# Values' products spread over the steps, value matrices loaded at the end of the bias stage, and six row buffers in an attention and two-layer expert kernel

## The chip, the cores and the metric

The kernel runs on one core of a Trainium2 chip. The metric is the device time of one execution in microseconds (us), the median over runs. Five engines work side by side, each through its own list of instructions in order: TensorE (PE, with its weight loads PEld), VectorE (DVE), ScalarE (ACT), GpSimd (POOL) and SyncE (SP). SP here does nothing but issue DMA transfers.

## The reference

Two batches, eight heads, 576 positions, head size 64. The attention scores get an additive bias that a small network computes from the distance of two positions; two layers of a 1152-token feed-forward block follow.

```
scores = scale * np.matmul(q, k.transpose(0, 1, 3, 2))
rel = (pos[:, None] - pos[None, :]).astype(np.float32)
psi_rel = np.log1p(np.abs(rel))
psi_i = np.log1p(np.maximum(pos[:, None].astype(np.float32), 1.0))
x = (psi_rel / psi_i)[..., None]
h = np.maximum(x @ w1 + b1, 0.0)
bias = h @ w2
scores = scores + bias.transpose(2, 0, 1)[None, :, :, :]
attn = np.exp(scores - np.max(scores, axis=-1, keepdims=True))
attn = attn / (np.sum(attn, axis=-1, keepdims=True) + 1e-09)
out = np.matmul(attn, v)
...
h = x @ w_in
g = h * (1.0 / (1.0 + np.exp(-1.702 * h)))
x = g @ w_out
...
h = x @ w_in
P = a[0] + a[1] * h + a[2] * h2 + a[3] * h3
Q = 1.0 + np.abs(b[0]) * np.abs(h) + np.abs(b[1]) * h2
out = (P / (Q + 1e-06)) @ w_out
```

## The kernel before

The order of all work is written out by hand; nothing reorders it. Each engine runs its own instructions in the order in which the code below emits them.

**Bias stage: beats.** The bias is made in 36 rows of 16 query positions (`A.rows`). A row goes through three functions, one beat apart. `bias_hidden` fills four hidden tiles (`room`) on DVE, POOL and ACT. `bias_matmul` multiplies them on PE into a PSUM tile, `wide` or `narrow`. `bias_out` copies the result to a tile `st` in SBUF with ACT (for three rows DVE, L141), mirrors the rest of the row with ACT, DVE or POOL, and SP writes `st` to the DRAM array `bias_all` (L152). `st` has four buffers: a fifth row waits until the write of the row four before it has landed. `beat()` is called from the step loop, with `FIRST[s]` saying how many beats stand ahead of step `s`, so that steps 0 to 9 lie between the beats. Beats also load the bias back for the steps (`bias_load`, tiles `bt`), prepare the first heads' queries and keys (`load_qk`, `q_high`, `k_low` and so on) and load the value matrices of the first three pairs (`load_v`).

**Attention: steps.** There are 40 steps. A step (`hp`, `b`, `qc`) is a pair of heads, a batch and one of five blocks of queries, in the order 4, 0, 1, 2, 3; block 4 has both heads in one tile, so half the matmuls. In step `s` PE does: the tail transposes of step `s - 3` (`tails`, L281 to L292, into a corner of the `wide` tiles that the scores of step `s` then use), the scores (L216), the other transposes of step `s - 3` into two PSUM tiles `pt`, and some parts of the values' products (`values`, L370 and L373). Scores use `wide`, of which there are two; DVE's L236 adds the bias, finds the extreme and frees the tile. ACT takes the exponentials (L240), copies `pt` to SBUF tiles `PT` (`evacuate`), and copies finished products (`xt`) to the input of the feed-forward block (L390); DVE's L395 makes the low part of these.

**Values.** A group is three blocks (4, 0, 1; 320 queries) or two (2, 3; 256 queries) of one pair of heads. When its last block has been evacuated, five parts are put on the list `pv`: parts 0 to 3 are two matmuls each (L370), part 4 is one (L373), after which the product is complete. The piece `pv` of a step takes parts from that list. From step 12 on it stands ahead of the evacuations in a step. Two `PT` tiles alternate, so the evacuations of a group wait for the products of the group two before it.

**Feed-forward.** From step 40 on the same loop lets the first hidden products of the feed-forward block (L485) start; its weights are split into two parts by `conv` pieces (L447 to L474), of which 14 stand in the attention steps listed in `CONVS`. The rest of the program is the feed-forward block (L485, L566, L573).

Of the kernel before, what the change touches and what calls it, by code (L numbers as in the profile page):

```python
# [24 lines left out]

QORDER = (4, 0, 1, 2, 3)
GROUPS = (((0, 256, 0), (512, 64, 256)), ((256, 256, 0),))
RLAG = 0

NFULL = 10  # L30

TLAG = 3
CONVS = (1,3,4,6,7,8,9,11,12,16,17,18,19,21)

FIRST = (19, 19, 21, 26, 30, 30, 39, 39, 39, 41, 41)

# [16 lines left out]
class Attention:  # L53
# [72 lines left out]

    def bias_out(self, r):
        nc = self.nc
        st = self.bp.tile([128, BW], F32, tag="st", name="st", bufs=4)
        c = int(self.rows.index(r) not in GP3)  # L130
        ps, left = self.bps.pop(r), 16 * r + 15
        n = ps.shape[1]

        if r < 18:
            side, other, image = st[:, left:], st[:, 0:left], st[:, 2 * left:left:-1]
        else:
            side, other, image = st[:, 0:n], st[:, n:], st[:, left - 1:left - (S - 16 * r):-1]
        i = self.rows.index(r)
        scale, bias = self.bc[:, C_NI + r:C_NI + r + 1], self.corr[:, c:c + 1]
        if i in (19, 28, 29):  # L140
            nc.vector.tensor_scalar(out=side, in0=ps, scalar1=scale, scalar2=bias, op0=ALU.mult, op1=ALU.add)  # L141
        else:
            nc.scalar.activation(out=side, in_=ps, func=AF.Identity, scale=scale, bias=bias)  # L143
        if i in (2, 3, 4, 7, 10, 13, 15, 18, 19, 21, 23, 24, 31, 32, 35):
            nc.scalar.copy(other, image)
        elif i in (8, 12, 14):
            nc.vector.tensor_copy(other, image)
        else:
            nc.gpsimd.tensor_scalar(out=other, in0=image, scalar1=1.0, scalar2=1.0, op0=ALU.mult, op1=ALU.mult)
# [34 lines left out]
        self.k[pb] = p.tile([128, 2, S], F32R, tag="k", name="k", bufs=bufs)  # L184

    def q_high(self, pb):
        self.nc.gpsimd.tensor_scalar(out=self.q[pb][:, 0, :], in0=self.raw[pb][:, 0:QW], scalar1=1.0, scalar2=1.0,
                                     op0=ALU.mult, op1=ALU.mult)

    def q_low(self, pb, a, b):  # L190
# [2 lines left out]
                                     op=ALU.subtract)  # L193

    def k_high(self, pb):
        self.nc.scalar.activation(out=self.k[pb][:, 0, :], in_=self.raw[pb][:, QW:], func=AF.Copy, scale=-0.125)

    def k_low(self, pb):
        k = self.k[pb]
        self.nc.vector.scalar_tensor_tensor(out=k[:, 1, :], in0=self.raw[pb][:, QW:], scalar=-0.125,  # L200
                                            in1=k[:, 0, :].bitcast(F32), op0=ALU.mult, op1=ALU.subtract)


# [90 lines left out]
    def tails_out(self, s):  # L294
        if not 0 <= s < len(self.steps):
            return
        hp, b, qc = self.steps[s]
        PTt = self.PT[hp, b, int(qc in (2, 3))][1]
        copy = self.nc.scalar.copy if qc in (() if hp else ()) else self.nc.vector.tensor_copy
        if qc < 4:  # L300
            o = 128 * (qc % 2)
            if isinstance(self.tl, list):
                for i in range(2):
                    copy(PTt[:, o + 64 * i:o + 64 * i + 64], self.tl[i])
            else:
                copy(PTt[:, o:o + 128], self.tl)
        else:
            for a in range(2):
                sl = slice(64 * a, 64 * a + 64)
                copy(PTt[sl, 256:320], self.tl[a][0:64, :])  # L310

    def transposes(self, s):
        self.evacuate(0)
        self.evacuate(1)
        if not 0 <= s < len(self.steps):
            return
        nc = self.nc
        hp, b, qc = self.steps[s]
        p = self.P.pop(s)
        off = 128 * (qc % 2) if qc < 4 else 256  # L320
        self.ev = (hp, b, int(qc in (2, 3))), qc, off, [], s < NFULL and qc < 4
        pts = self.ev[3]
        for i in range(2):
            pt = self.pt.tile([128, 512], F32, tag=f"pt{i}", name="pt", bufs=1)
            pts.append(pt[:].rearrange("p (a c q) -> p a c q", a=2, c=4))
        for a in range(2 if qc < 4 else 1):
            for c in range(4):
                x = p[:, a, 128 * c + 64 * a:128 * c + 64 * a + 128]
                if qc == 4:
                    for i in range(2):  # L330
                        sl, o = slice(64 * i, 64 * i + 64), 128 * c + 64 * i
                        nc.tensor.transpose(pts[i][:, a, c, :], p[sl, a, o:o + 128], self.ident[sl, sl], tile_position=(64 * i, 0))
                elif s < NFULL:
                    nc.tensor.transpose(pts[a].rearrange("p a c q -> p (a c q)")[:, 128 * c:128 * c + 128], x, self.ident)  # L334
                else:
                    self.flip([pt[:, a, c, :] for pt in pts], x)


    def evacuate(self, i):
        if self.ev is None:  # L340
# [5 lines left out]
        copy = nc.scalar.copy if i or qc in eva else nc.vector.tensor_copy  # L346
# [7 lines left out]
        if i and qc in (1, 3):  # L354
            self.pv += [(grp, c) for c in range(5)]
        self.ev = None if i else self.ev


    def values(self, grp, c):
# [17 lines left out]
    def values_out(self):  # L377
        nc = self.nc
        if self.xt is None:
            return  # L380
        (hp, b, g), n, xt = self.xt
        self.xt = None
        for q, m, o in GROUPS[g]:
            end = b * S + q + m
            while m:
                ci, i = divmod(end - m, CH)
                w = min(m, CH - i)
                hi, lo = self.x[ci]
                self.xlo.append((lo[:, hp, i:i + w], xt[:, o:o + w], hi[:, hp, i:i + w]))
                nc.scalar.copy(hi[:, hp, i:i + w], xt[:, o:o + w])  # L390
                m, o = m - w, o + w

    def values_lo(self):
# [5 lines left out]
class Moe:  # L399
# [68 lines left out]
    def split(self):  # L468
        if self.ready:
            nc = self.nc  # L470
            w, o, val, j = self.ready
            self.ready = None
            nc.scalar.copy(w[:, 2 * o, :], val)  # L473
# [103 lines left out]
def attention_moe_moe(tc, t):  # L577
# [50 lines left out]
    def beat():  # L628
# [20 lines left out]
            A.k_high(i // 10)  # L649
        if i in (7, 14):  # L650
            A.k_low(i // 10)
        if i in (21, 26, 34):
            A.load_v((21, 26, 34).index(i))
        if i in (14, 16, 18, 22):
            A.load_qk(2, (14, 16, 18, 22).index(i))
        if i == 7:
# [14 lines left out]
    g, nh = {}, 0  # L671
    for s in range(n + TLAG + 2):
        prep = []
        while s <= 10 and beats[0] < FIRST[s]:
            beat()
        if s < n:
# [14 lines left out]
        else:  # L691
            A.values_out()
            A.values_lo()
            A.tails(s - TLAG)
        if s == n:
            A.ps.release()
# [11 lines left out]
        for piece in (('ea','eb','xa','to','qh','ql','kh','xb','su','cv','pv','tr','no','vo','kl','vl') if s < 12 else ('tr','vo','to','pv','qh','ea','ql','kh','eb','xa','xb','su','no','kl','vl','cv')):  # L708
            if piece == 'ea':
                A.evacuate(0)  # L710
            elif piece == 'eb':
                A.evacuate(1)
            elif piece == 'su':
                A.sums(s - 1)
            elif piece == 'to':
# [27 lines left out]
            elif piece == 'tr':  # L743
                A.transposes(s - TLAG)
            elif piece == 'pv':
                for _ in range(5 if s >= n or len(pv) > 5 else 2 if pv and pv[0][1] == 0 else 3):
                    if pv and s >= 10:
                        A.values(*pv.pop(0))
                if s == n + TLAG + 1 and 1:
# [247 lines left out]
```

## Time and profile before

| | before |
|---|---|
| median of 3 runs | 595.82 us (595.65 to 596.84) |
| profiled execution | 597.2 us, span 595.3 us |
| PE busy | 569.3 us (96% of the span) |
| ACT, DVE, POOL busy | 439.9, 422.5, 379.6 us |
| chain that ended last | PE 78%, DVE 7%, ACT 6%, DMA 4%, POOL 3%, issue 2% |

Busy shares are averages over stages with different limits. The bias stage takes the span's first 75 us or so, the attention steps without beats run to about 179 us, and the feed-forward block takes the rest. In the rows further down, the first number of a timeline row is the start in us from the span's start.

### The profile page before, as it was taken

The page shows a single profiled execution, that of the slowest core. Times are in us where ns is not written, and L with a number is a line of the kernel's source. Part 1 is how long each engine was busy: PE and PEld are TensorE (multiplying, and loading weights), DVE is VectorE, ACT ScalarE, POOL GpSimd, SP SyncE. Part 2 cuts the span into 40 slices and gives each one's busy share as a digit, 9 for nine tenths or more (in the row PEclk, how much of TensorE's full clock was granted, in tenths as well). Part 3 has the DMA queues.
Part 4 walks back from the last instruction along what each step waited for, and adds up shares of the span by engine and source line. Part 5 has one row for each costly group of instructions (what it writes and reads, how often), then busy time and mean ns, then how long its engine had stood idle before and what let it go on. Part 6 is the DMA issues. An engine that isn't in the chain of part 4 may idle for free.

```text
span 595.3 us, 10998 instructions
## 1 busy us (share of the span) xinstructions
PE 569.3 (96%) x3815; PEld 480.1 (81%) x3815; DVE 422.5 (71%) x919; ACT 439.9 (74%) x929; POOL 379.6 (64%) x431
## 2 busy tenths in 40 slices
PE   6986999999999999999999999999999999999997
PEld 2233466666666999999999999988898989999995
DVE  7987775688876886565655737678998666657663
ACT  7987777898987675555545536779999887888783
POOL 5957554577755775546554646759888665656563
PEclk9987999999999999999999999999999999999999
DMA  5789760834514564343443414501200100010001
GB/s 170 208 277 283 223 247 2 317 133 143 196 59 142 177 196 150 115 130 123 139 126 122 139 41 138 179 1 35 72 1 1 54 1 2 0 37 19 0 1 53
DMA packets 23911, 66.25 MB, mean 111 GB/s; under 512 B 2480, under 2 KB 3376, under 8 KB 23856
## 3 DMA queue, kind: packets, MB, share of 16 engines
q1 hardware_dynamic: 23712, 65.43, 34.0%
q8 instruction: 30, 0.49, 0.3%
q14 instruction: 25, 0.20, 0.1%
q10 hardware_dynamic: 144, 0.13, 0.1%
HBM read 52.30 MB, written 13.25 MB: 110 GB/s over the span
## 4 chain that ended last, share of the span: by engine, by line
PE 78%; DVE 7%; ACT 6%; DMA 4%; POOL 3%; issue 2%; SPq 0%; ACTq 0%; POOLq 0%; DVEq 0%
PE hps L485 30%; PE acc L566 16%; PE acc L573 15%; PE wide L216 5%; PE xt L370 4%; DVE p L236 3%; PE wide L123 2%; DMA bt<-bias_all 2%; PE pt L334 1%; PE pt L292 1%; PE xt L373 1%; DMA bias_all<-st 1%; PE narrow L123 1%; PE wide L292 1%; ACT st L143 1%
## 5 line engine op out<-in xcount | busy, mean ns | idle before, releaser
L485 PE MATMUL hps<-xhi,w 128*128 128x384 f32 x768 | 150.8, 337 | 0.9 <-DVE part L547 0.9
L485 PEld LDWEIGHTS hps<-xhi,w 128*128 128x128 f32 x768 | 135.6, 188 | 6.7 <-DVE part L547 2.7
L497 POOL TENSOR_TENSOR glo<-sg,ghi 128x384 fp32r<-128x384 f32 x48 | 49.0, 1020 | 72.5 <-PE acc L566 50.0
L474 POOL TENSOR_TENSOR w<-tmp,w 128x512 fp32r<-128x512 f32 x64 | 85.4, 1334 | 10.4 <-ACT w L473 10.0
L252 POOL TENSOR_SCALAR p<-p,mn 128x576 f32<-128x576 f32 x72 | 59.0, 829 | 47.0 <-DVE mn L250 39.6
L485 PE MATMUL hps<-xlo,w 128*128 128x384 f32 x384 | 82.0, 334 | 0.0
L566 PE MATMUL acc<-ghi,w 128*128 128x384 f32 x384 | 78.4, 334 | 0.1
L573 PE MATMUL acc<-w,ghi 128*128 128x512 f32 x288 | 75.8, 393 | 0.0
L485 PEld LDWEIGHTS hps<-xlo,w 128*128 128x128 f32 x384 | 68.0, 188 | 0.0
L566 PEld LDWEIGHTS acc<-ghi,w 128*128 128x128 f32 x384 | 67.6, 188 | 0.4 <-DVE xlo L395 0.4
L504 DVE TENSOR_TENSOR sg<-hps,sg 128x384 f32<-128x384 f32 x48 | 26.7, 557 | 51.9 <-ACT sg L503 51.9
L544 POOL TENSOR_SCALAR ra<-ra,small 128x384 f32<-128x384 f32 x48 | 28.2, 587 | 55.1 <-ACT ra L529 55.0
L240 ACT ACTIVATE p<-p,mn 128x576 f32<-128x576 f32 x72 | 55.7, 779 | 9.7 <-DVE mn L236 9.5
L573 PEld LDWEIGHTS acc<-w,ghi 128*128 128x128 f32 x288 | 53.4, 188 | 8.6
L236 DVE CUSTOM_DVE_ANT_0 p<-wide,bt 128x576 f32<-128x576 f32 x72 | 52.3, 751 | 9.3 <-PE wide L216 6.3
L494 ACT CAST ghi<-sg 128x384 fp32r<-128x384 f32 x48 | 24.7, 514 | 43.3 <-PE acc L566 27.2
L546 POOL TENSOR_TENSOR ra<-ra,part 128x384 f32<-128x384 f32 x48 | 49.9, 1039 | 4.0
L216 PE MATMUL wide<-k,q 64*128 64x288 f32 (+1 forms) x432 | 46.2, 318 | 2.2 <-ACT st L143 1.7
L503 ACT ACTIVATE sg<-hps 128x384 f32<-128x384 f32 x48 | 23.5, 489 | 30.6 <-PE hps L485 30.6
L566 PE MATMUL acc<-glo,w 128*128 128x384 f32 x192 | 45.0, 334 | 0.0
L447 ACT ACTIVATE up<-raw 128x512 int32<-128x512 uint32 x59 | 37.5, 636 | 7.5 <-DVE tmp L463 6.6
L573 PE MATMUL acc<-w,glo 128*128 128x512 f32 x144 | 42.5, 393 | 0.0
(115 smaller groups left out, 1158.3 us busy)
## 6 DMA issues: line engine op xcount, KB each, us to landing
raw<-win SPq DMA_DIRECT2D x32, 512.0 KB, 3.6
raw<-wout SPq DMA_DIRECT2D x32, 512.0 KB, 3.5
bias_all<-st SPq DMA_DIRECT2D x36, 295.5 KB, 3.7
bt<-bias_all SPq DMA_DIRECT2D x16, 576.0 KB, 5.9
qk<-qk SPq DMA_DIRECT2D x7, 608.0 KB, 6.3
v<-v SPq DMA_DIRECT2D x8, 320.0 KB, 5.6
out<-o SPq DMA_DIRECT2D x8, 256.0 KB, 2.2
bt<-bias_all SPq DMA_DIRECT2D x8, 144.0 KB, 3.6
```

What stands on the lines that cost most here:

```text
L216: nc.tensor.matmul(ps[:, half, 0:288], q[p, x, 128 * qc:128 * qc + 128], k[p, y, 288 * half:288 * half + 288], start=(i == 0), stop=(i == ...
L236: nc.vector.tensor_tensor_reduce(out=pv.rearrange("p (x j) -> p x j", x=2), in0=ps[:, :, 0:288], in1=self.bt[qc][:, a, :].rearrange("p (x ...
L240: nc.scalar.activation(out=pv, in_=pv, func=AF.Exp, bias=mn[:, a:a + 1], scale=-1.0, accum_out=mn[:, 2 + 2 * a:3 + 2 * a])
L252: nc.gpsimd.tensor_scalar(out=p[:, a, :], in0=p[:, a, :], scalar1=mn[:, 8 + a:9 + a], scalar2=1.0, op0=ALU.mult, op1=ALU.mult)
L447: nc.scalar.activation(out=self.up[j].bitcast(I32), in_=lo, func=AF.Copy, scale=2.0 ** -29)
L474: nc.gpsimd.tensor_tensor(out=w[:, 2 * o + 1, :], in0=val, in1=w[:, 2 * o, :].bitcast(F32), op=ALU.subtract)
L485: nc.tensor.matmul(ps[:, 0:CH], w[:, wi, 128 * d:128 * d + 128], xx[:, d, :], start=(i == 0 and d == 0), stop=(i == 2 and d == 3))
L497: nc.gpsimd.tensor_tensor(out=glo[:], in0=g, in1=ghi[:].bitcast(F32), op=ALU.subtract)
L544: nc.gpsimd.tensor_scalar(out=t0[0][:], in0=t0[0][:], scalar1=self.pb[:, 1:2], scalar2=1.000001, op0=ALU.mult, op1=ALU.add)
L546: nc.gpsimd.tensor_tensor(out=t0[0][:], in0=t0[0][:], in1=t0[1][:], op=ALU.add)
L566: nc.tensor.matmul(acc[e][:, 0:CH], w[:, wi, 128 * e:128 * e + 128], g[gi][:], start=(first and i == 0), stop=(last and i == 2))
L573: nc.tensor.matmul(acc[e][:], g[gi][:, 128 * e:128 * e + 128], w[:, wi, :], start=(first and i == 0), stop=(last and i == 2))
```

## The change

Four things change, beside a number of switches that are added and left off (`KLE`, `QHE`, `TACT` and so on), and a bookkeeping list in `evacuate` that leaves the order as it was.

```
-        st = self.bp.tile([128, BW], F32, tag="st", name="st", bufs=4)
+        st = self.bp.tile([128, BW], F32, tag="st", name="st", bufs=6)
...
-        if i in (21, 26, 34):
-            A.load_v((21, 26, 34).index(i))
+        if i in (38, 39, 40):
+            A.load_v((38, 39, 40).index(i))
...
-                for _ in range(5 if s >= n or len(pv) > 5 else 2 if pv and pv[0][1] == 0 else 3):
+                for _ in range(5 if s >= n else 3 if len(pv) > 5 else 2):
                     if pv and s >= 10:
                         A.values(*pv.pop(0))
...
-CONVS = (1,3,4,6,7,8,9,11,12,16,17,18,19,21)
+CONVS = (1, 3, 4, 5, 6, 7, 8, 9, 11, 12, 16, 17, 18, 19, 21)
```

Rows for the bias wait on the write of the row six before them, no longer four. The three value loads move behind the rows. In the steps, `CONVS` gets one more place, so the last pieces of the fifth weight half stand one place earlier and the last place is empty.

The first place is PE's list in three attention steps in a row, with blocks 4, 0 and 1 (`wide<-k,q` are the scores, `x6` those of block 4; `128x64 x2` into `wide` the tails; `pt` the other transposes; `64x320 x4` two parts of a group's products, `xt<-PTt,v` its part 4; a product counts here once, in the profile's counts twice). Before:

```order
L292 MATMUL wide<-cst,p 128x64 x2
L216 MATMUL wide<-k,q 128x288 x6
L292 MATMUL pt<-cst,p 128x64 x16
L292 MATMUL wide<-cst,p 128x64 x2
L216 MATMUL wide<-k,q 128x288 x12
L292 MATMUL pt<-cst,p 128x64 x16
L370 MATMUL xt<-PT,v 64x320 x4
L292 MATMUL wide<-cst,p 128x64 x2
L216 MATMUL wide<-k,q 128x288 x12
L292 MATMUL pt<-cst,p 128x64 x16
L370 MATMUL xt<-PT,v 64x320 x4
L373 MATMUL xt<-PTt,v 128x320
```

And with the change, the same steps in a later turn of the pattern, once it has settled (L308 is L292 of before, L232 is L216, L389 and L392 are L370 and L373):

```order
L308 MATMUL wide<-cst,p 128x64 x2
L232 MATMUL wide<-k,q 128x288 x6
L308 MATMUL pt<-cst,p 128x64 x16
L392 MATMUL xt<-PTt,v 128x256
L308 MATMUL wide<-cst,p 128x64 x2
L232 MATMUL wide<-k,q 128x288 x12
L308 MATMUL pt<-cst,p 128x64 x16
L389 MATMUL xt<-PT,v 64x320 x4
L308 MATMUL wide<-cst,p 128x64 x2
L232 MATMUL wide<-k,q 128x288 x12
L308 MATMUL pt<-cst,p 128x64 x16
L389 MATMUL xt<-PT,v 64x320 x4
```

Part 4 of the two-block group has moved into the step of block 4, which had no products, and part 4 of the three-block group has left the step of block 1 for that of block 2. In turns of five steps (blocks 4, 0, 1, 2, 3) the parts were 0, 2, 3, 2, 3 and are 1, 2, 2, 3, 2.

The second place is SP's list at the end of the bias stage (`bias_all<-st` are the rows, `bt<-bias_all` the bias for a step, `v<-v` the value matrices). Before:

```order
L159 DMA bt<-bias_all 128x2x576
L152 DMA bias_all<-st 16x8x591 x3
L179 DMA v<-v 128x640
L152 DMA bias_all<-st 16x8x591 x4
L159 DMA bt<-bias_all 128x2x576
L174 DMA qk<-qk 128x1216 x2
L159 DMA bt<-bias_all 128x2x576 x3
```

With the change:

```order
L168 DMA bt<-bias_all 128x2x576
L161 DMA bias_all<-st 16x8x591 x7
L188 DMA v<-v 128x640
L168 DMA bt<-bias_all 128x2x576
L188 DMA v<-v 128x640 x2
L183 DMA qk<-qk 128x1216 x2
L168 DMA bt<-bias_all 128x2x576 x3
```

All three value loads now stand behind the last row, two of them behind the `bt` load that waits for the last row to land, and ahead of two `qk` loads.

## Rows read from the trace of the kernel before

**Rows 1.** Busy time in stretches: stretch, length, PE, PEld, DVE, ACT, POOL, clock, DMA, GB/s.
```profile
20.00:42.00 22.00, 18.79 (x135) 6.71 (x134) 19.37 (x45) 18.20 (x38) 15.49 (x27) 0.92 0.87 267
51.00:64.05 13.05, 10.48 (x79) 5.74 (x75) 8.50 (x24) 7.32 (x18) 8.06 (x13) 0.61 0.76 236
81.50:104.73 23.23, 23.00 (x207) 15.22 (x209) 13.13 (x52) 17.82 (x44) 12.32 (x17) 1.00 0.22 75
120.01:135.31 15.30, 14.38 (x173) 10.13 (x174) 13.05 (x49) 14.11 (x37) 11.65 (x13) 1.00 0.29 107
197.77:595.30 397.53, 392.44 (x2106) 371.68 (x2106) 269.90 (x467) 277.13 (x562) 252.78 (x254) 1.00 0.23 76
```

**Rows 2.** Waits of ACT, 20 to 75 us: us in total, times, longest.
```profile
ACT st L143 <- DMA bias_all<-st: 2.3, 3, 1.3
```

**Rows 3.** Timeline of ACT: start, us, instruction, count, idle before and its releaser.
```profile
52.32 0.66 ACT L143 ACTIVATE st<-wide,corr,bc 128x368 f32<-128x368 f32 x1 [1.30 <-DMA bias_all<-st]
```

**Rows 4.** Timeline of PE in the bias stage.
```profile
50.55 0.85 PE L123 MATMUL narrow<-room,bc 128*32 128x384 f32 x8 [1.33 <-ACT st L143]
...
53.03 0.31 PE L281 MATMUL wide<-cst,p 64*64 64x64 f32 x1 [1.46 <-ACT st L143]
53.03 1.86 PE L216 MATMUL wide<-k,q 64*128 64x288 f32 x12
56.00 1.56 PE L123 MATMUL wide<-room,bc 128*32 128x400 f32 x8 [1.11 <-DVE PTt L310]
...
58.52 1.86 PE L216 MATMUL wide<-k,q 64*128 64x288 f32 x12
...
71.03 1.07 PE L216 MATMUL wide<-k,q 64*128 64x288 f32 x12
```

**Rows 5.** Timeline of DVE in the bias stage.
```profile
54.96 0.76 DVE L236 CUSTOM_DVE_ANT_0 p<-wide,bt 128x576 f32<-128x576 f32 x1 [2.30 <-POOL st L149]
...
57.83 0.70 DVE L141 TENSOR_SCALAR st<-wide,bc,corr 128x400 f32<-128x400 f32 x1 [0.68 <-DMA bias_all<-st]
```

**Rows 6.** Timeline of SP, the DMA issues at the end of the bias stage.
```profile
67.11 0.59 SPq L179 DMA_DIRECT2D v<-v  x1
...
75.21 0.36 SPq L159 DMA_DIRECT2D bt<-bias_all  x1
75.63 0.94 SPq L174 DMA_DIRECT2D qk<-qk  x2
```

**Rows 7.** DMA issues of the page: count, KB each, median us to landing.
```profile
bt<-bias_all SPq DMA_DIRECT2D x16, 576.0 KB, 5.9
v<-v SPq DMA_DIRECT2D x8, 320.0 KB, 5.6
```

**Rows 8.** Timeline of PE: the first products, and five steps from 120 us.
```profile
83.11 2.37 PE L370 MATMUL xt<-PT,v 128*64 128x320 f32 x16
...
120.01 1.09 PE L216 MATMUL wide<-k,q 64*128 64x288 f32 x12
...
122.96 1.10 PE L216 MATMUL wide<-k,q 64*128 64x288 f32 x12
...
126.50 1.04 PE L216 MATMUL wide<-k,q 64*128 64x288 f32 x12
...
128.98 0.24 PE L292 MATMUL wide<-cst,p 64*128 64x64 f32 x1 [0.19 <-DVE mn L236]
129.66 0.24 PE L292 MATMUL wide<-cst,p 64*128 64x64 f32 x1 [0.43 <-DVE mn L224]
...
135.31 0.24 PE L292 MATMUL wide<-cst,p 64*128 64x64 f32 x1 [0.26 <-DVE mn L224]
```

**Rows 9.** The chain that ended last: start, us, what; two last parts of products.
```profile
125.78 0.74 PE xt L373 x2
...
132.26 0.63 PE xt L373 x2
```

**Rows 10.** Timeline of PE where the steps end.
```profile
180.72 0.30 PE L284 MATMUL tl<-cst,p 128*128 128x128 f32 x1 [1.19 <-DVE xlo L395]
```

More of the change, by code (lines that the diff above doesn't have):

```diff
@@ L27 @@
 GROUPS = (((0, 256, 0), (512, 64, 256)), ((256, 256, 0),))
-RLAG = 0
+MIRA = (2, 3, 4, 7, 10, 13, 15, 18, 19, 21, 23, 24, 31, 32, 35)
+MIRD = (8, 12, 14)
+EVB = (19, 28, 29)
+KLE = 0
+QHE = 0
+KHE = 0
+TACT = ()
+EVD = ()
+XHE = 0
+WHE = 0
 NFULL = 10
 TLAG = 3
-CONVS = (1,3,4,6,7,8,9,11,12,16,17,18,19,21)
+CONVS = (1, 3, 4, 5, 6, 7, 8, 9, 11, 12, 16, 17, 18, 19, 21)
 FIRST = (19, 19, 21, 26, 30, 30, 39, 39, 39, 41, 41)
@@ L143, in bias_out @@
             nc.scalar.activation(out=side, in_=ps, func=AF.Identity, scale=scale, bias=bias)
-        if i in (2, 3, 4, 7, 10, 13, 15, 18, 19, 21, 23, 24, 31, 32, 35):
+        if i in MIRA:
             nc.scalar.copy(other, image)
-        elif i in (8, 12, 14):
+        elif i in MIRD:
             nc.vector.tensor_copy(other, image)
@@ L186, in q_high @@
     def q_high(self, pb):
-        self.nc.gpsimd.tensor_scalar(out=self.q[pb][:, 0, :], in0=self.raw[pb][:, 0:QW], scalar1=1.0, scalar2=1.0,
+        if QHE == 1 and pb > 2:
+            self.nc.scalar.copy(self.q[pb][:, 0, :], self.raw[pb][:, 0:QW])
+            return
+        (self.nc.vector if QHE == 2 and pb > 2 else self.nc.gpsimd).tensor_scalar(out=self.q[pb][:, 0, :], in0=self.raw[pb][:, 0:QW], scalar1=1.0, scalar2=1.0,
                                      op0=ALU.mult, op1=ALU.mult)
@@ L195, in k_high @@
     def k_high(self, pb):
+        if KHE and pb > 2:
+            (self.nc.vector if KHE == 2 else self.nc.gpsimd).tensor_scalar(out=self.k[pb][:, 0, :], in0=self.raw[pb][:, QW:], scalar1=-0.125, scalar2=1.0,
+                                     op0=ALU.mult, op1=ALU.mult)
+            return
         self.nc.scalar.activation(out=self.k[pb][:, 0, :], in_=self.raw[pb][:, QW:], func=AF.Copy, scale=-0.125)
@@ L199, in k_low @@
         k = self.k[pb]
-        self.nc.vector.scalar_tensor_tensor(out=k[:, 1, :], in0=self.raw[pb][:, QW:], scalar=-0.125,
+        (self.nc.gpsimd if KLE and pb > 2 else self.nc.vector).scalar_tensor_tensor(out=k[:, 1, :], in0=self.raw[pb][:, QW:], scalar=-0.125,
                                             in1=k[:, 0, :].bitcast(F32), op0=ALU.mult, op1=ALU.subtract)
@@ L298, in tails_out @@
         PTt = self.PT[hp, b, int(qc in (2, 3))][1]
-        copy = self.nc.scalar.copy if qc in (() if hp else ()) else self.nc.vector.tensor_copy
+        copy = self.nc.scalar.copy if qc in TACT and s >= NFULL else self.nc.vector.tensor_copy
         if qc < 4:
@@ L312, in transposes @@
     def transposes(self, s):
-        self.evacuate(0)
-        self.evacuate(1)
+        self.evacuate(0, s + TLAG)
+        self.evacuate(1, s + TLAG)
         if not 0 <= s < len(self.steps):
@@ L321, in transposes @@
         self.ev = (hp, b, int(qc in (2, 3))), qc, off, [], s < NFULL and qc < 4
-        pts = self.ev[3]
+        pts, self.left = self.ev[3], [0, 1]
         for i in range(2):
@@ L336, in transposes, with evacuate @@
                     self.flip([pt[:, a, c, :] for pt in pts], x)
-    def evacuate(self, i):
-        if self.ev is None:
+    def evacuate(self, i, s):
+        if self.ev is None or i not in self.left:
             return
@@ L345, in evacuate @@
         eva = (0, 1, 2, 3, 4) if grp[0] else (2, 3, 4)
-        copy = nc.scalar.copy if i or qc in eva else nc.vector.tensor_copy
+        copy = nc.vector.tensor_copy if qc not in eva and not i or s >= NFULL and qc in EVD and not i else nc.scalar.copy
         if full:
@@ L353, in evacuate @@
             copy(PT[:, :, :, off + 64 * i:off + 64 * i + 64], pts[i])
-        if i and qc in (1, 3):
+        self.left.remove(i)
+        if self.left:
+            return
+        self.ev = None
+        if qc in (1, 3):
             self.pv += [(grp, c) for c in range(5)]
-        self.ev = None if i else self.ev
     def values(self, grp, c):
@@ L389, in values_out @@
                 self.xlo.append((lo[:, hp, i:i + w], xt[:, o:o + w], hi[:, hp, i:i + w]))
-                nc.scalar.copy(hi[:, hp, i:i + w], xt[:, o:o + w])
+                (nc.vector.tensor_copy if XHE else nc.scalar.copy)(hi[:, hp, i:i + w], xt[:, o:o + w])
                 m, o = m - w, o + w
@@ L472, in split @@
             self.ready = None
-            nc.scalar.copy(w[:, 2 * o, :], val)
+            (nc.vector.tensor_copy if WHE and not self.hs else nc.scalar.copy)(w[:, 2 * o, :], val)
             nc.gpsimd.tensor_tensor(out=w[:, 2 * o + 1, :], in0=val, in1=w[:, 2 * o, :].bitcast(F32),
@@ L673, in attention_moe_moe @@
         prep = []
+        order = ('ea', 'eb', 'xa', 'to', 'qh', 'ql', 'kh', 'xb', 'su', 'cv', 'pv', 'tr', 'no', 'vo', 'kl', 'vl') if s < 12 else ('tr', 'vo', 'to', 'pv', 'qh', 'ea', 'ql', 'kh', 'eb', 'xa', 'xb', 'su', 'no', 'kl', 'vl', 'cv')
         while s <= 10 and beats[0] < FIRST[s]:
@@ L695, in attention_moe_moe @@
         if s == n:
+            assert not fs
             A.ps.release()
@@ L707, in attention_moe_moe @@
             A.xp = new(name="xt", bufs=1, space=PSUM, reuse_waits="tile")
-        for piece in (('ea','eb','xa','to','qh','ql','kh','xb','su','cv','pv','tr','no','vo','kl','vl') if s < 12 else ('tr','vo','to','pv','qh','ea','ql','kh','eb','xa','xb','su','no','kl','vl','cv')):
+        for piece in order:
             if piece == 'ea':
-                A.evacuate(0)
+                A.evacuate(0, s)
             elif piece == 'eb':
-                A.evacuate(1)
+                A.evacuate(1, s)
             elif piece == 'su':
```

2 lines of the change are left out of this document (1 added, 1 removed).

## The prediction, made before the changed kernel ran

> **What bounds the kernel now.** I read the page's busy shares first (PE 96% of the span), then the stretches, because shares average over stages with different limits. [rows 1] shows four of these. From about 198 us on PE is busy 392.44 of 397.53 us; that is the feed-forward block, which the change does not touch. So a microsecond that PE gains ahead of it is a microsecond at the end, and nothing else counts. Ahead of it, in 20 to 42 us DVE is the fullest engine (19.37 of 22.00) with the DMA engines at a busy share of .87. In 51 to 64 us nobody is full: DVE 8.50 and PE 10.48 of 13.05, at a mean granted clock of .61. In 81.5 to 104.7 us PE is busy 23.00 of 23.23. In 120.0 to 135.3 us, one whole turn of five attention steps, PE is busy 14.38 and ACT 14.11 of 15.30. Where PE is already full, a new order of its work gains nothing; where it waits, there are .9 us in a turn.
>
> Next I read the waits. ACT waits three times for the write of an older `st` to land, 2.3 us in all, 1.3 at the longest [rows 2], and DVE once, .68 us [rows 5]. Then the timelines around the longest wait and around PE's waits in the steps [rows 3, 4, 5, 8], the issues on SP [rows 6], and the chain that ended last for the price of the moved parts [rows 9].
>
> **Six buffers.** Two of ACT's three waits, 1.0 us of the 2.3, fall in the stretch in which DVE is full, so I count them at nothing. The third is the one at 52.32 [rows 3]: the bias row is evacuated 1.30 late, PE's tails and scores wait 1.46 for it at 53.03 [rows 4], and DVE's addition of the bias at 54.96 has been idle for 2.30 [rows 5]. A fifth and sixth buffer let this row go ahead at once.
>
> A second effect comes with it. PE has idled 1.33 and 1.46 there, and after that its clock is at the lower of its two levels (1.2 of 2.4 GHz; mean .61 of the stretch). A score group then takes 1.86 and not the 1.07 of 71.03, and the wide bias product 1.56 [rows 4], where half of that, .78, is my estimate for the full clock. If the wait goes and the clock stays up, the gain is 1.30 + 2 x (1.86 - 1.07) + .78 = 3.7 us. If the clock falls anyway, it is 1.3: the wait of 1.33 at 50.55 for ACT's earlier copy, and the 1.11 for DVE at 56.00, are not the buffers' doing. The ceiling is DVE's idle time there, 13.05 - 8.50 = 4.55, since DVE's work would then fill the stretch. I cannot tell which of the two clocks it will be, and take 2.8, a little above the middle of 1.3 and 3.7, because the .68 of DVE at 57.83 goes too.
>
> **Value loads.** Three loads of 320 KB move from among the rows to the end of them. Where they were, the DMA engines were at .87 and 267 GB/s [rows 1]; two of them are 640 KB, 2.4 us of that stream. But DVE is full in that stretch, and the loads are not what it waits for, so I take 0; the bounds are 0 and 2.4 gained. The Trainium skill, "Perfetto Trace Analysis", section "Roofline", says that one active core is bounded by its 16 DMA engines at some 435 GB/s together. By that page the stream at 267 GB/s has room and the move is worth nothing; by the busy share of .87 it has little, and the move could be worth the 2.4. No run here has shown yet which of the two holds, for transfers of this shape.
>
> In their new place they must be in time. One stands ahead of the last `bt` load, two behind it, that is behind 75.6 us, and ahead of the two `qk` loads of 75.63 [rows 6]. The first product of the groups is at 83.11 [rows 8], and `v<-v` takes 5.6 us to land in the median [rows 7]: issued at about 76 they land at 82, with about one microsecond to spare, and what the first products need is the first of them, with 2 or 3 more. The two issues of SP cost about .6 each (.59 at 67.11), which puts the `qk` loads 1.2 later; `bt` at 5.9 to landing is as long. Cost 0, provided that this cover holds; if it is gone, what is late is PE's first products at step 10, and behind them everything on PE, since its list is in order.
>
> **Values' parts in the steps.** In turns of five steps the parts change from 0, 2, 3, 2, 3 to 1, 2, 2, 3, 2. In the turn of [rows 8] PE waits twice for DVE in the step after the block-2 scores (.19 and .43, the tails into `wide` wait until the bias has been added to the tile two before) and once in the step of block 4 (.26): .88 in 15.30, near the .92 that busy time leaves [rows 1]. The mechanism is that PE is too quick where a step holds few products, and too slow where it holds three. Part 4 of the three-block group (.74) and of the two-block group (.63) are the ones that move [rows 9]. The .74 goes from the step of block 1 to that of block 2, ahead of the waits of .19 and .43, and covers these .62. The .63 goes from the step of block 3 to the one of block 4, and covers the .26. What the giving steps lose is the risk: the step of block 1 lasts 126.50 - 122.96 = 3.54 with the part, 2.80 without; the step of block 0, with two parts and nothing more, lasts 122.96 - 120.01 = 2.95, so about .15 of new wait arises. .88 - .15 = .7 in a turn. ACT then becomes the next bound: 14.11 busy of a turn of 14.6 leaves .5 of room, so I take .6.
>
> From 104.7 to 178.7 us there are 74 / 15.30 = 4.8 turns: 4.8 x .6 = 2.9, taken as 2.8. Steps 10 to 15 bring nothing, because PE is at 23.00 of 23.23. Bounds: 1.0, when ACT gives back most of it (its waits for `pt` are then one after another), and 4.7, all of PE's idle time from 81.5 to 178.7: .23 + 4.8 x .92.
>
> New waits: two `PT` tiles alternate, and products now finish later, so two evacuations (at about step 10 and at step 18) wait on ACT for a part that PE does in the same step. What is queued behind on ACT are the exponentials, for which PE's transposes wait three steps later; by the room of .5 in a turn a delay of 1 us is absorbed in two turns. Bounds 0 to 1, taken as 0. At the steps' end, the tail at 180.72 waits 1.19 for DVE's low part of a finished product [rows 10]; with the last part elsewhere this wait moves by a step and a like one of about 1 us arises. I take 0 for it, with -.7 and +.3 as ends. The `conv` pieces that move one place up are the same pieces; the place they leave empty and the place they take lie beside a full PE: 0.
>
> **Sum.** 2.8 + 2.8 = 5.6 us, of the span of 595.3: 589.7. The profiled execution of before took 597.2, 1.9 more than its span and 1.4 more than the median of the runs shown, 595.82. Taken off the median: **590.2 us**, faster by 0.95%.
>
> **The rivals.**
> - *The steps are bound by ACT, not by PE's waits.* ACT is busy 14.11 of 15.30 [rows 1], and its copies of `pt` come in pairs. For: PE's idle time is short, and ACT's share is close behind. Against: the waits of [rows 8] name DVE, whose busy time is 13.05. Then only the bias stage gains: 595.8 - 2.8 = 593.0. Chance .15.
> - *The bias stage is bound by its DMA stream, so more buffers only move the wait.* For: share .87, then .76 [rows 1]; the write of a row lands late for that reason. Against: DVE is nearly full in the first stretch, and in the second a wait of 1.3 stands alone. Then only the steps gain: 593.0 as well. Chance .13.
> - *Neither does anything:* DVE's addition of the bias is the pace in both stages and idle time comes back elsewhere. 595.8. Chance .08.
> - *Slower: the values come late.* A `v` issued at 76 must land before 83.1. If the loads queue behind each other and behind the writes, so that the first lands after about 84, PE stands at its first product with nothing else in its list. A stop of 1.5 us is the kind of wait behind which the clock fell at 53 us; ten microseconds of PE at half clock then cost up to 5 more. 1.5 + 5 - 5.6 = +.9, or 596.7; with the steps' gain halved, 598. From landing times of about 8 us on it decides. Chance .08.
>
> **How the numbers follow.** The forecast, both gains in part or whole, has .56 and its own range from the bounds of the two terms, less their extremes together: 588.0 to 592.5. The two rivals at 593.0 hold .28, and with their own scatter reach to about 594.3. Below, the ceiling of both terms (4.55 + 4.7 = 9.2, 586.6) is unlikely at once; 587.3 leaves out some .04. So 587.3 to 594.3 leaves out .04 below and about .15 above (the two last rivals). A measurement of this kernel tells about 0.2%, 1.2 us, from no change: faster than 594.6 .82, between 594.6 and 597.0 .10, slower .08.
>
> **What would show it.** Six buffers: no wait of ACT or DVE for `bias_all<-st` beyond some tenths, and the clock of the stretch 51 to 64 us near 1 (right) or again near .6 (then 1.3 is what is left). The loads: the first product no later after its step's scores than before, no wait of PE for a DMA at step 10; the share of DMA in 20 to 42 us lower, with DVE's busy share unchanged if the loads are worth nothing. Steps: a turn of 14.6 to 14.8, PE's waits of .43 and .26 gone, and none above .2 in the step of block 1. Rows that name ACT as the releaser of PE's waits in place of DVE would speak for the first rival. It would be wrong altogether if the feed-forward block began at the same time as before, or if an evacuation's wait for products came back in every turn.

## The result, and the profile after

| | before | after |
|---|---|---|
| median | 596.33 us (595.65 to 597.42, 4 runs) | 591.83 us (591.60 to 592.36, 4 runs) |
| profiled execution, span | 597.2, 595.3 us | 592.4, 590.4 us |
| PE busy | 569.3 us | 567.0 us |

The changed kernel is faster: ratio 0.9915, 95% interval 0.9898 to 0.9933, which is 4.0 to 6.1 us; the medians differ by 4.5. The forecast was 5.6 us, which lies inside this interval.

The stretches of the changed kernel, with the columns of [rows 1]; the last three are three whole turns of five steps, from block 4 to block 4, of steps 20 to 24, 25 to 29 and 30 to 34:

```profile
20.00:42.00 22.00, 18.72 (x134) 6.65 (x128) 19.19 (x44) 17.83 (x37) 15.66 (x27) 0.95 0.84 254
51.00:64.05 13.05, 11.32 (x99) 4.94 (x98) 12.45 (x30) 10.73 (x24) 11.37 (x20) 1.00 0.85 265
81.50:104.73 23.23, 23.23 (x244) 15.92 (x244) 13.18 (x56) 17.96 (x47) 13.08 (x17) 1.00 0.35 117
104.70:120.00 15.30, 15.30 (x184) 10.45 (x186) 12.15 (x46) 13.77 (x37) 9.77 (x12) 1.00 0.87 330
193.30:590.40 397.10, 391.72 (x2101) 370.55 (x2100) 269.41 (x466) 278.03 (x562) 252.86 (x253) 1.00 0.24 76
112.04:127.77 15.73, 15.09 (x182) 10.42 (x180) 13.63 (x50) 14.69 (x39) 11.63 (x13) 1.00 0.50 177
127.77:142.52 14.75, 14.45 (x174) 10.25 (x173) 12.16 (x48) 13.62 (x35) 10.74 (x13) 1.00 0.42 136
142.52:158.12 15.60, 14.53 (x175) 10.20 (x173) 14.05 (x53) 14.99 (x38) 11.99 (x14) 1.00 0.54 195
```

In 51 to 64 us the clock is 1.00 and not .61, and DVE is now nearly full (12.45 of 13.05, before 8.50). From 81.5 to 120 us PE does not wait at all. But the three turns are not alike. The same three turns of the kernel before were equally long, and yet not equally loaded (the columns are the same, DVE the third and ACT the fourth of the busy times):

```profile
117.73:133.03 15.30, 14.17 (x175) 10.05 (x173) 12.72 (x49) 14.73 (x39) 11.43 (x14) 1.00 0.42 145
133.03:148.33 15.30, 14.38 (x175) 10.14 (x173) 11.79 (x44) 12.94 (x33) 10.99 (x13) 1.00 0.43 133
148.33:163.62 15.29, 14.37 (x175) 10.04 (x173) 13.25 (x50) 15.11 (x40) 11.87 (x15) 1.00 0.56 197
```

The feed-forward block is as it was.

PE's timeline where before it waited 1.33, 1.46 and 1.11 [rows 4]:

```profile
50.88 0.85 PE L132 MATMUL narrow<-room,bc 128*32 128x384 f32 x8 [1.34 <-ACT st L152]
51.66 0.53 PE L297 MATMUL wide<-cst,p 64*64 64x64 f32 x2
51.95 1.09 PE L232 MATMUL wide<-k,q 64*128 64x288 f32 x12
54.17 0.88 PE L132 MATMUL wide<-room,bc 128*32 128x400 f32 x8 [1.14 <-DVE PTt L326]
...
55.64 1.51 PE L232 MATMUL wide<-k,q 64*128 64x288 f32 x12
...
67.69 1.08 PE L232 MATMUL wide<-k,q 64*128 64x288 f32 x12
```

The middle wait is gone, the other two are as long as before, and the clock stays up through both. The scores of 71.03 now stand at 67.69: 3.3 us gained in this one place. ACT and DVE wait for no write of `st` any more.

The starts of the scores of some steps, from PE's timelines, show where time is gained and given back (`b_buf6` and `b_parts` are experiments below):

| start of, us | before | after | gained | b_buf6 | b_parts |
|---|---|---|---|---|---|
| step 3 | 44.37 | 44.70 | -.3 | 44.13 | 44.71 |
| step 6 | 71.03 | 67.69 | 3.3 | 67.10 | 70.19 |
| step 10 | 81.76 | 78.51 | 3.3 | 78.16 | 80.92 |
| step 15 | 101.37 | 96.58 | 4.8 | 97.77 | 98.97 |
| step 20 | 117.73 | 112.04 | 5.7 | 114.12 | 114.42 |
| step 25 | 133.03 | 127.77 | 5.3 | 129.42 | 130.18 |
| step 30 | 148.33 | 142.52 | 5.8 | 144.72 | 144.91 |
| step 35 | 163.62 | 158.12 | 5.5 | 160.01 | 160.46 |
| step 39 | 175.56 | 169.59 | 6.0 | 171.94 | 171.97 |
| first of feed-forward | 184.4 | 179.0 | 5.4 | 180.8 | 181.4 |
| end of span | 595.3 | 590.4 | 4.9 | 591.6 | 592.5 |

Each column is one execution. `b_parts` stands .8 ahead of before at step 6, where its edit has done nothing yet; by so much can two executions differ.

### The profile page after: what moved, and what is told of

It is laid out like the page before. It is cut to its first block, busy times and chain, and to the rows that moved or that the text cites. A ratio compares the mean times of both kernels' runs of the same rounds, so it can differ in the third digit from the quotient of the medians.

```text
span 590.4 us, 10985 instructions
## 1 busy us (share of the span) xinstructions
PE 567.0 (96%) x3815; PEld 478.8 (81%) x3815; DVE 424.1 (72%) x919; ACT 440.0 (75%) x929; POOL 380.6 (64%) x431
## 4 chain that ended last, share of the span: by engine, by line
PE 73%; DVE 10%; POOL 6%; ACT 5%; DMA 3%; issue 3%; SPq 0%; DVEq 0%; POOLq 0%; ACTq 0%
PE hps L504 29%; PE acc L592 15%; PE acc L585 14%; PE wide L232 4%; PE xt L389 4%; DVE p L252 2%; POOL room L108 2%; DVE tmp L482 1%; PE pt L308 1%; DMA bt<-bias_all 1%; PE pt L350 1%; PE xt L392 1%; DMA bias_all<-st 1%; DVE tmp L472 1%; PE narrow L132 1%
## 5 line engine op out<-in xcount | busy, mean ns | idle before, releaser
L493 POOL TENSOR_TENSOR w<-tmp,w 128x512 fp32r<-128x512 f32 x64 | 85.4, 1335 | 13.0 <-ACT w L492 12.7
L232 PE MATMUL wide<-k,q 64*128 64x288 f32 (+1 forms) x432 | 44.8, 309 | 1.7 <-ACT st L152 1.2
```

What stands on the lines that cost most here:

```text
L232: nc.tensor.matmul(ps[:, half, 0:288], q[p, x, 128 * qc:128 * qc + 128], k[p, y, 288 * half:288 * half + 288], start=(i == 0), stop=(i == ...
```

## The experiments

**b_buf6, b_vlate, b_parts: each part of the change alone.** The edits to the kernel before, in this order:

```
-        st = self.bp.tile([128, BW], F32, tag="st", name="st", bufs=4)
+        st = self.bp.tile([128, BW], F32, tag="st", name="st", bufs=6)
```
```
-        if i in (21, 26, 34):
-            A.load_v((21, 26, 34).index(i))
+        if i in (38, 39, 40):
+            A.load_v((38, 39, 40).index(i))
```
```
-                for _ in range(5 if s >= n or len(pv) > 5 else 2 if pv and pv[0][1] == 0 else 3):
+                for _ in range(5 if s >= n else 3 if len(pv) > 5 else 2):
...
-CONVS = (1,3,4,6,7,8,9,11,12,16,17,18,19,21)
+CONVS = (1, 3, 4, 5, 6, 7, 8, 9, 11, 12, 16, 17, 18, 19, 21)
```

> The kernel before with six st buffers, nothing else. Theory (the wait for the write and the half clock behind it): the wait of 1.30 us at 52 us goes, the clock of 51 to 64 us is near 1, and the kernel is 3.0 to 3.5 us faster than before (ratio about 0.9945). Rival (the value loads are what keeps the writes late; more buffers only move the wait): less than 1 us faster, with another wait of ACT or DVE for bias_all<-st left and a clock still near 0.6.

> The kernel before with the three value loads behind the rows, four buffers. Theory (the loads are not what the stage waits for): within 0.7 us of before, the wait at 52 us is still there. Rival (the DMA stream of the stage is the bound, 640 KB of it taken out): 1 to 2.4 us faster, and the waits for bias_all<-st are shorter by a third or more. A second rival, slower: the values' first product waits for its load, by 1 us or more.

> The kernel before with the new rule for the values' parts and the conv place, nothing else. Theory as in the prediction (PE's waits for DVE in every turn are covered): 2.8 us faster, ratio 0.995, turns of 14.6 to 14.8 us. Theory formed on the changed kernel's trace (only a one-off gain while the parts that are late fill PE's waits, and turns in which ACT is the bound gain nothing): 1.3 to 2.0 us faster, turns alternate between about 14.8 and 15.5. Rival: nothing.

Measured: `b_buf6` 593.38 us, ratio .9952 (.9939 to .9965), 2.9 us, a little under what was expected; `b_vlate` 596.43, ratio 1.0002 (.9991 to 1.0013), nothing; `b_parts` 594.49, ratio .9968 (.9955 to .9980), 1.9 us, as the theory formed on the changed kernel's trace had it and not the prediction's 2.8. In `b_buf6` the stretch of 51 to 64 us has the clock 1.00, and no wait for a write is left:

```profile
51.00:64.05 13.05, 11.30 (x99) 5.11 (x95) 12.62 (x29) 10.67 (x24) 11.44 (x20) 1.00 0.89 277
```

In `b_vlate` the busy share of the DMA engines in 20 to 42 us falls from .87 to .82 while DVE stays at 19.35 of 22.00, and PE waits for no value matrix. ACT's waits for writes are 1.1 us there and not the 2.3 of before, which the rival had asked for, but no time came of it. The parts add up: 2.9 + 0 + 1.9 = 4.8, within the whole's interval.

**a_buf4, a_vearly: the same two from the other side**, in the changed kernel.

```
-        st = self.bp.tile([128, BW], F32, tag="st", name="st", bufs=6)
+        st = self.bp.tile([128, BW], F32, tag="st", name="st", bufs=4)
```
```
-        if i in (38, 39, 40):
-            A.load_v((38, 39, 40).index(i))
+        if i in (21, 26, 34):
+            A.load_v((21, 26, 34).index(i))
```

> The changed kernel with four st buffers again. Theory: it loses what six buffers gave, 3.0 to 3.5 us, so 1.4 to 2.0 us faster than before is left, and the clock of the stretch around 51 to 64 us is low again. Rival (with the value loads out of the way four buffers are enough): within 1 us of the changed kernel.

> The changed kernel with the value loads at their old beats. Theory: within 0.7 us of the changed kernel, 4.2 to 5.2 us faster than before. Rival (six buffers help only because the loads are out of the way): 1.5 us or more slower than the changed kernel, and a wait for bias_all<-st is back.

Measured: `a_buf4` 594.84, ratio to before .9965 (.9952 to .9978), so 1.3 to 2.9 us are left. In 51 to 64 us the clock is .74, and PE waits .73 at 52.48 for a row that ACT copies at 51.77. The profile puts ACT's own wait of .58 there down to a row of PE; the write of the row four before, issued at 45.48, took 6.2 us to land, so it landed at 51.7 and fits as what ended that wait. `a_vearly` 592.13, ratio .9927 (.9913 to .9941), as the changed kernel. Six buffers do not need the loads out of the way, and the loads out of the way do not spare the buffers.

**b_fill: the wait left in, PE's idle time filled.**

```
-            for g in range(4):
+            for g in [*range(4)] * {22: 2, 23: 3}.get(r, 1):
                 w, h = self.bc[:, C_W2 + 32 * g:C_W2 + 32 * g + 32], tiles[g]
```

> The kernel before with four buffers, in which PE multiplies the bias row of width 368 twice and the one of width 384 three times into the same tile, so that PE has 2.4 us more to do where it idles 1.33 and 1.46 at 49 to 53 us; the row's wait for the write stays. The products are the same. Theory (the idle time lets the clock fall, and the clock is the larger part of the gain of six buffers): the clock of 51 to 64 us is near 1, score groups at 53 and 58 us take about 1.1 and not 1.86, and the kernel is 1.5 to 2.5 us faster although PE does more. Rival (the wait itself is all that counts, the clock's price is hidden behind DVE and ACT): within 0.7 us of before, or slower.

PE's timeline of this kernel:

```profile
48.50 1.42 PE L123 MATMUL wide<-room,bc 128*32 128x368 f32 x16
50.63 2.14 PE L123 MATMUL narrow<-room,bc 128*32 128x384 f32 x24 [0.71 <-ACT st L143]
...
52.76 1.03 PE L216 MATMUL wide<-k,q 64*128 64x288 f32 x12
...
56.45 1.54 PE L216 MATMUL wide<-k,q 64*128 64x288 f32 x12
...
68.53 1.06 PE L216 MATMUL wide<-k,q 64*128 64x288 f32 x12
```

ACT still waits .80 for the write, but the clock of 51 to 64 us is 1.00 and the scores of step 6 come at 68.53, 2.5 us ahead of the profiled execution of before. The timing over 12 runs shows much less: 595.23 against 596.24, but these runs fall into two clumps (seven from 594.73 to 595.24, five from 596.03 to 596.79), and the comparison of all of them gives the ratio .9995 (.9984 to 1.0006), which is not told from no change. The 1.5 to 2.5 us of the theory did not come; the rival's "within 0.7" stands. So the profiled execution of before could be an untypical one, and the next two runs look at that.

**b_same1, b_same2: the kernel before, unchanged, looked at twice more.**

> The kernel before again, unchanged. Theory (the clock's fall behind PE's waits at 49 to 53 us comes in some executions for long and in others hardly, which is why times with four buffers scatter over 3 us and with six over less than 1): the clock of 51 to 64 us is another than 0.61 where the time is another than 597.2 us, about 1 us of time for each 0.13 of that clock, and the wait of about 1 us for the write is there whatever the clock. Rival (the clock falls the same way each time): 0.6 again, whatever the time.

> The kernel before once more, unchanged, as a second look at the same question. Theory: the clock of 51 to 64 us goes with the time (near 1 at about 594.8 us, near 0.6 at about 597.2 us). Rival: 0.6 again, whatever the time.

The stretch of 51 to 64 us in `b_same1`, and PE's timeline there:

```profile
51.00:64.05 13.05, 10.26 (x94) 4.79 (x95) 11.98 (x29) 10.64 (x23) 10.38 (x19) 1.00 0.91 278
```
```profile
51.54 0.85 PE L123 MATMUL narrow<-room,bc 128*32 128x384 f32 x8 [1.33 <-ACT st L143]
...
53.07 0.24 PE L281 MATMUL wide<-cst,p 64*64 64x64 f32 x1 [0.50 <-ACT st L143]
53.07 1.08 PE L216 MATMUL wide<-k,q 64*128 64x288 f32 x12
```

ACT's copy of the waiting row there, and below it the one of `b_same2`; before, it started at 52.32 [rows 3]:

```profile
52.35 0.66 ACT L143 ACTIVATE st<-wide,corr,bc 128x368 f32<-128x368 f32 x1 [0.35 <-DMA bias_all<-st]
52.38 0.66 ACT L143 ACTIVATE st<-wide,corr,bc 128x368 f32<-128x368 f32 x1 [1.02 <-DMA bias_all<-st]
```

The same stretch in `b_same2`, and its wait:

```profile
51.00:64.05 13.05, 10.54 (x84) 5.18 (x84) 9.76 (x25) 8.61 (x20) 8.83 (x15) 0.74 0.82 263
```
```profile
53.09 0.25 PE L281 MATMUL wide<-cst,p 64*64 64x64 f32 x1 [1.17 <-ACT st L143]
53.09 1.39 PE L216 MATMUL wide<-k,q 64*128 64x288 f32 x12
```

Put beside each other, with three other executions with four buffers, and with the starts of the scores of steps 3, 4 and 6 taken apart:

| execution | PE's wait at 53 us | step 3 at | step 3 to 4 | clock 51 to 64 us | step 4 to 6 | time, us |
|---|---|---|---|---|---|---|
| before, first profile | 1.46 | 44.37 | 8.66 | .61 | 18.00 | 597.2 |
| b_same2 | 1.17 | 44.72 | 8.37 | .74 | 17.41 | 596.77 |
| b_parts | 1.12 | 44.71 | 8.31 | .74 | 17.17 | other steps |
| a_buf4 | .73 | 44.55 | 7.93 | .74 | 17.75 | other steps |
| b_vlate | .83 | 44.71 | 8.04 | .87 | 16.56 | 595.73 |
| b_same1 | .50 | 45.41 | 7.66 | 1.00 | 15.76 | 595.12 |
| b_fill | none | 44.46 | 8.30 | 1.00 | 15.77 | 594.73 |
| b_buf6 | none | 44.13 | 7.24 | 1.00 | 15.73 | 593.43 |

(`b_parts` and `a_buf4` differ from before in later steps too, so their times are left out.) The two prices come apart. From step 3 to step 4 stands the wait for the write: .4 to 1.4 us over `b_buf6`, in `b_fill` perhaps in part the filling itself. From step 4 to step 6 stands the clock: nothing where it is 1.00, .8 at .87, 1.4 to 2.0 at .74, 2.3 at .61. So the theory holds in kind, with a price nearer .8 us for .13 of the clock than 1.

The wait itself is not constant, but not because the write lands at another moment: the waiting copy started at 52.32, 52.38 and 52.35 in before, `b_same2` and `b_same1`, the same kernel each time, and the write that it waits for had been issued at 45.32, 45.68 and 45.85 and taken 6.9, 6.6 and 6.4 us to land. What differs is how early the engines stand there. `b_same1` came 1 us later, its clock having been down earlier (.52 in 40 to 46 us, against .84 and 1.00), and so it waited only .50 and kept its clock afterwards.

The timings bear the clock out in part. Of the 29 runs of before that were timed beside the first four experiments, the ten with the lowest mean clock over the whole span (.991 or less) took 596.57 to 597.75 us and the three with 1.00 594.84 to 595.05. But in `b_fill`, whose mean clocks are .993 and above, both clumps have clocks of .996 and .997. What sets those two clumps apart is not shown.

**a_khe: ScalarE relieved in the steps.**

```
-KHE = 0
+KHE = 1
```
```
         if KHE and pb > 2:
             (self.nc.vector if KHE == 2 else self.nc.gpsimd).tensor_scalar(out=self.k[pb][:, 0, :], in0=self.raw[pb][:, QW:], scalar1=-0.125, scalar2=1.0,
                                      op0=ALU.mult, op1=ALU.mult)
             return
```

> The changed kernel in which GpSimd and not ScalarE makes the high part of the keys for the last five pairs (0.69 us of ScalarE in each turn of five steps). PE's list is the same. Theory (in the turns of the first batch ACT is the bound, with 15.0 of 15.6 us busy): these turns get shorter by 0.3 to 0.6 each, 0.6 to 1.5 us faster than the changed kernel. Rival (DVE's or POOL's chain sets those turns): no gain, or a loss, with PE's waits put down to POOL's normalisation.

Measured: 592.45, ratio .9931 (.9917 to .9945), no gain. The turns of steps 30 to 34 and 25 to 29:

```profile
142.26:157.84 15.58, 14.54 (x174) 10.22 (x172) 14.02 (x52) 14.56 (x38) 12.63 (x15) 1.00 0.55 196
127.58:142.26 14.68, 14.39 (x174) 10.21 (x172) 12.16 (x48) 13.14 (x34) 11.36 (x14) 1.00 0.44 136
```

ACT has .4 less to do in the first of them, and it is as long as before the edit (15.58 against 15.60). So ACT's busy time alone does not set this turn, and the rival is the likelier. As POOL has .6 more to do there (12.63, before the edit 11.99), the run does not say whether DVE or POOL does: in both kernels PE waits .4 for each of them in this turn.

**a_drain: no late parts at step 16.**

```
-                for _ in range(5 if s >= n else 3 if len(pv) > 5 else 2):
+                for _ in range(5 if s >= n or s < 16 else 3 if len(pv) > 5 else 2):
```

> The changed kernel in which steps 10 to 15 take all parts that are ready, as before, so that no products are late when the turns begin. Theory (the gain up to 120 us comes from late parts that fill PE's waits, once): PE waits again about 0.6 to 1.1 us between step 15 and step 20, and 0.5 to 1.1 us of the gain is lost against the changed kernel. Rival (the even split itself covers those waits in each turn): no difference from the changed kernel beyond 0.4 us.

Measured: 592.71, ratio .9938 (.9923 to .9953); beside `a_vearly`, on the same chip, .6 slower by the medians, though the two intervals overlap. In 99 to 113 us PE is busy 13.60 of 14.11, with one wait of .5 for DVE, which fits the theory, at its lower end. Its turns of steps 25 to 29 and 30 to 34 show the even split without anything late:

```profile
128.69:142.91 14.22, 14.22 (x174) 10.18 (x172) 11.68 (x44) 13.02 (x34) 10.69 (x13) 1.00 0.45 143
142.91:158.50 15.59, 14.56 (x174) 10.22 (x173) 14.03 (x52) 14.96 (x38) 11.98 (x14) 1.00 0.55 194
```

A turn of the second batch is 1.1 us shorter than the 15.30 of before and PE is full in it; a turn of the first batch is .3 longer. The chain that ended last in the changed kernel says what differs: in the second batch's turn (130 to 141 us) its long pieces are PE's alone, in the first batch's (141 to 158) DVE's additions and then 6 us of POOL, and in the first batch's turn before that (ahead of 128 us) DVE's additions and conversion pieces (`tmp`):

```profile
123.45 0.76 DVE p L252
...
125.16 1.00 DVE tmp L467
...
128.62 0.97 DVE tmp L472
130.93 0.86 PE wide L232 x12
132.27 1.23 PE xt L389 x8
...
147.30 0.67 DVE p L252
150.67 0.67 DVE p L252
151.81 2.32 POOL p L268 x2
154.13 0.92 POOL w L493
155.34 1.07 POOL q L204
156.40 1.47 POOL p L268 x2
```

`CONVS` counts back from step 40: steps 21 to 24 and 31 to 34, both of the first batch, hold four conversion pieces each, steps 25 to 29 two.

**a_conv, a_conv2: the conversion pieces elsewhere.** In `a_conv` most go to the second batch's turns, in `a_conv2` three to each turn of the first batch and four to each of the second, counted from the list (the expectation says three in each).

```
-CONVS = (1, 3, 4, 5, 6, 7, 8, 9, 11, 12, 16, 17, 18, 19, 21)
+CONVS = (1, 2, 3, 4, 5, 10, 11, 12, 13, 14, 15, 16, 20, 21, 22)
```
```
-CONVS = (1, 3, 4, 5, 6, 7, 8, 9, 11, 12, 16, 17, 18, 19, 21)
+CONVS = (1, 2, 4, 5, 6, 9, 10, 11, 12, 14, 15, 16, 19, 20, 21)
```

> The changed kernel with the conversion pieces of the weights (DVE 0.75, 1.18 and 0.69 us each, ScalarE 0.7 and 0.6) out of the steps of the first batch, 31 to 34 and 21 to 23, and in those of the second batch instead. PE's list is the same. Theory (DVE is the bound of the first batch's turns: 9.22 of 9.40 us busy in three steps at 146 to 156 us): the turn of steps 30 to 34 takes 14.4 to 14.9 and not 15.60 us, and that of 25 to 29, which gets the pieces, 15.0 to 15.6 and not 14.75; the whole is within 0.8 us of the changed kernel. Rival (the turn of the first batch is long for another reason, as the parts' places): it stays at 15.5 or more.

> The changed kernel with the fifteen conversion pieces spread over all turns, three in each, in the steps after which DVE has least to do (none in the step that makes the low part of the keys, few ahead of it). PE's list is the same. Theory (a conversion piece on DVE makes the step behind it 3.2 to 3.4 us long where PE needs 2.7 to 3.0): turns of 14.4 to 15.0 us in both batches, 0.6 to 1.5 us faster than the changed kernel. Rival (what is saved in one turn comes back in the next, as where the pieces went to the second batch): within 0.5 us of the changed kernel.

Measured: `a_conv` 591.40, ratio .9923 (.9907 to .9938); `a_conv2` 591.65, ratio .9922 (.9906 to .9937). Three turns of `a_conv`, steps 20 to 24, 25 to 29 and 30 to 34:

```profile
111.11:126.34 15.23, 15.22 (x182) 10.56 (x180) 12.22 (x48) 14.34 (x38) 11.29 (x13) 1.00 0.46 164
126.34:141.36 15.02, 14.51 (x174) 10.23 (x172) 13.99 (x51) 14.36 (x36) 12.26 (x13) 1.00 0.48 155
141.36:156.55 15.19, 14.41 (x174) 10.18 (x173) 12.63 (x48) 14.09 (x37) 11.16 (x13) 1.00 0.49 180
```

The length moves with the pieces: step 34, now without one ahead of it, takes 2.74 and not 3.24 us, step 31, now behind one, 3.40 and not 2.95. The turn of 30 to 34 gets .4 shorter, less than the .7 expected at least (step 30 has a piece now), and the turn of 25 to 29 .3 longer. In `a_conv2` steps 25 to 29 take 14.69 and steps 30 to 34 15.05. From step 10 to step 39 both take 90.4 us against 91.1 of the changed kernel, and their times cannot be told from its. So the conversion pieces make these steps long, but what they cost in one turn mostly comes back in the other. Which engine it is that they hold up is not separated, because a piece has work on DVE, ACT and POOL (L493 in the chain above). DVE is the fullest, with 9.22 of 9.40 us at 146 to 156 us in the changed kernel; POOL stands in the chain behind it, and no run moved POOL's work alone.

## Why the prediction was right, and where not

- **Six buffers, 2.8 us:** 2.9 measured alone (2.1 to 3.6). The two parts of the term were the right ones, the wait and the clock behind it. That the two earlier waits cost nothing fits: step 3 starts at 44.13 in `b_buf6` and 44.70 in the changed kernel, against 44.37 to 45.41 with four buffers. But the agreement is in part luck. The clock stayed up, and for that case the prediction had 3.7; against the profiled execution of before, on which it was worked out, `b_buf6` does gain 3.7 (spans of 595.3 and 591.6). What the prediction did not see is that this was one execution in which the clock had fallen long. Others lose less, and 2.8, chosen between the two cases because the clock could not be told, met the median of them. The wait costs .4 to 1.4 us and the clock nothing to 2.3. Of the sizes inside the term two were off: at the full clock the second score group takes 1.51 (55.64), not 1.07, and the wide product .88 (54.17), not .78.
- **Value loads, 0:** shown from both sides. The sentence on the Trainium skill's page "Perfetto Trace Analysis", section "Roofline", comes out on the side of the measurement: the move was worth nothing. That the stream at 267 GB/s had room is borne out by other stretches, 278 GB/s in 51 to 64 us of `b_same1` and 330 in 104.7 to 120 of the changed kernel, but by `b_vlate` alone it is not shown, because DVE is full in 20 to 42 us and would hide it. The busy share of .87 was no sign of a bound: 267 and 330 GB/s both stand beside it. The cover of the loads held: they land in 4.7 us in the median and no product waits for one.
- **Parts, 2.8 us:** 1.9 alone (1.2 to 2.7); the waits for DVE were the right ones, but the term was too large, and the interval leaves the 2.8 out. From step 10 to step 39 the gain is in fact 2.7 us (93.8 to 91.1), but not as the prediction worked it out. The step that failed is ".6 in each of 4.8 turns", worked out from one turn that lies across both batches. Turns alternate: 15.60 (longer by .3), 14.75 (shorter by .55), so that from step 20 to step 39 only .3 is gained. Nor was "steps 10 to 15 bring nothing" right. Parts put off there let PE run ahead by 1.5 us, and in steps 15 to 19 another .9 is gained, where they fill the waits:

```profile
104.70:120.00 15.30, 14.18 (x174) 10.02 (x174) 10.88 (x44) 12.88 (x36) 8.54 (x11) 1.00 0.94 330
```

  That is before; with the change PE is busy 15.30 of 15.30 there. The parts are made up in steps 20 to 24, which are .4 longer. `a_drain` puts this at .6 to .9 us by the medians. That the whole's 5.6 still lies in the interval of 4.0 to 6.1 is no support for this term.
- **The tail.** Forecast was a like wait of about 1 us in another step, at 0. It came, and some of the gain is given back there:

```profile
173.26 0.30 PE L300 MATMUL tl<-cst,p 128*128 128x128 f32 x1 [1.07 <-DVE xlo L414]
...
174.13 0.70 PE L392 MATMUL xt<-PTt,v 128*128 128x256 f32 x2
...
175.36 0.71 PE L308 MATMUL pt<-cst,p 64*128 64x64 f32 x15 [0.21 <-ACT PT L369]
...
176.27 2.37 PE L389 MATMUL xt<-PT,v 128*64 128x320 f32 x16 [0.20 <-PE pt L308]
```

  The wait of 1.19 [rows 10] is replaced by 1.07 + .21 + .20, and the .70 of a part 4 that before lay ahead of that wait (178.09, the wait ending at 180.72) now stands behind it: 6.0 us ahead at step 39, 5.4 at the first product of the feed-forward block. The three waits explain .3 of these .5 to .6. Another .5 is lost behind it, of which a wait of .2 for DVE at 208 us is named; the rest stays open, and the changed kernel's spans themselves differ by .8.
- **The rivals.** "The steps are bound by ACT, not by PE's waits" was half right: the first batch's turns did get no shorter, but relieving ACT gave nothing (`a_khe`), and the conversion pieces are what makes them long (`a_conv`), by DVE or POOL. The DMA stream as the bound is ruled out by `b_buf6`, which gained with the loads in place, and by `b_vlate`; late values by `b_vlate` and the changed kernel.

## What to carry to other kernels

Read the load of each engine in more than one turn of a loop before multiplying by the number of turns. Here the turns of before were equally long and unequally loaded, and side work that is placed by a table (the conversion pieces) made every other turn long once PE's waits were gone. Count what is still owed at a mark along the way, since a list that puts work off looks like a gain until it is paid, and some of it is paid behind the last wait. And where the clock has fallen in the profiled execution, look at a second one before pricing it: the same wait cost .4 us in one execution of this kernel and 1.4, with 2.3 of the clock behind it, in another.

## What was not expected of the hardware

The times scatter more with four buffers. Of the kernels with four, 29 runs of before spread over 2.9 us (594.84 to 597.75) and 8 to 12 runs of the others over 2.1 to 3.1. Of those with six, 4 to 6 runs each spread over .4 to 1.8, `b_buf6` over .8 (592.99 to 593.76). The numbers of runs differ, so the ranges are only a rough guide.

Part of the scatter is PE's clock. It stayed at 2.4 GHz with waits of PE of 1.33 and .50 in a row (`b_same1`), and with 1.34 and 1.14 some 3 us apart (the changed kernel). It fell to 1.2 GHz behind 1.33 and 1.46 (before), 1.33 and 1.17 (`b_same2`), 1.33 and 1.12 (`b_parts`), 1.33 and .83 (`b_vlate`) and 1.33 and .73 (`a_buf4`). The length of the second wait alone does not order them: the mean of 51 to 64 us was .87 behind the .83 and .74 behind the .73. In `b_same1` the clock had fallen ahead of the wait; PE came later, waited less, and the clock did not fall behind it.
